# Issuing the float32 DFT matmuls of a fused FFT and MLP kernel in pairs

## The chip, the cores and the metric

The kernel runs on one core of a Trainium2 chip. The metric is the device time of one execution in microseconds (us). The engines are named as in the profile: PE (matmul), PEld (PE's weight loads), DVE (vector), ACT (activation), POOL (GpSimd) and SP, which issues the DMAs.

## The reference

A circular convolution along the sequence (by a real FFT, a product with a filter, and the inverse FFT) for 8 batches of 3008 x 256, and behind it a two-layer MLP with a rational activation on all 24064 rows.

```python
X = np.fft.rfft(x, axis=1)
Y = X * (filt_r + 1j * filt_i)[None, :, :]
y = np.fft.irfft(Y, n=x.shape[1], axis=1)
...
h = x @ w_in                      # 256 -> 2048
h2 = h * h; h3 = h2 * h
P = a[0] + a[1] * h + a[2] * h2 + a[3] * h3
Q = 1.0 + np.abs(b[0]) * np.abs(h) + np.abs(b[1]) * h2
return (P / (Q + 1e-06)) @ w_out  # 2048 -> 256
```

## The kernel before, in words

The FFT of length 3008 = 64 x 47 is made of small DFT matmuls in float32. Of one batch, stage 1 has 16 matmuls of 47 points (tiles `s`, 8 steps `q` with two halves `j` each, 96 x 512), stage 2 has 12 forward matmuls of 64 points (tiles `y`) and 12 inverse ones (tiles `z`), and stage 3 brings the result back with 47 points (tiles `x`, chunks of 5 small matmuls) and splits it into a high and a low part, `xh` and `xl`. The MLP's matmuls are fp32r with operands split into such parts.

The MLP goes in 752 units: 47 row tiles of 512 rows times 16 slices f of the hidden layer. The function `pipeline` has one step per unit. The engines run in the order in which it issues. In step i it issues, for PE, the six matmuls of `h` of unit i (L437, L438, L440: `product_in`), then at most one piece of convolution, then six matmuls `o` (L520 to L522: `product_out`) of the unit five steps back. Two of these are special: at f = 5 of each row tile no `o` is issued, since the two banks of `o` are still being copied out (`oe`), and at f = 6 there are two units' worth of `o`. A "step f" below is a step whose number is f modulo 16.

The elementwise work of a unit is spread over the later steps by `ORDER`: on DVE a step has g_hi of the unit two back (L497), then the DVE work of the convolution piece, then `rest` of the unit three back (L505), `p` of the last unit (L488) and g_lo of the unit three back (L511, which writes `lo_u`). At the end of the steps with f = 4 DVE also copies half of the last tile's output (`oe`, L250).

Convolution of batch b+1 runs while the MLP works on batch b. A generator (`stage1`, `stage2`) yields a price before each matmul (0.86), `pipeline` lets it go on when a credit is above zero, and the credit grows by 0.38 a step (0.6 for batch 1). After the matmul the generator yields; its evacuation is issued in the same step behind the first three names of `ORDER`. Pieces of stage 3 come in at f = 2 and 3 or f = 10 and 11, or a step later.

Six PSUM banks serve `h`, `s`, `y`, `z` and `x`. `Banks.tile` takes the free bank with the smallest key; `Banks.done` gives it back with the key "step + 0.5" for the convolution (issued with its evacuation) and "step + 1" for a unit, whose bank is given back at its g_lo, three steps after its `product_in`. So in every step four banks belong to units once `product_in` has taken its own, and two are free for the convolution. PE waits at a matmul until the last reader of the bank's former tile has finished.

Of the kernel before, what the change touches and what calls it, by code (L numbers as in the profile page):

```python
# [9 lines left out]
F32 = mybir.dt.float32  # L10
# [3 lines left out]
ALU = mybir.AluOpType  # L14
# [12 lines left out]
C = 256  # L27
# [13 lines left out]
WAITS = (0, 1)  # L41
ORDER = [('g_hi', 2), ('act3', 1), ('act0', 0), ('act4', 1), ('act2', 0), ('act1', 0), ('rest', 3), ('p', 1), ('g_lo', 3), ('pool_m', 2), ('pool_q1', 1), ('pool_q0', 0)]
EV1, EV2, EVO = "A", "AV", "AV"
# [14 lines left out]
TT = 512  # L58
# [45 lines left out]
def conv_moe(ctx: ExitStack, tc: tile.TileContext, xp, fr, fi, w_in, w_out, ab, mats, small, sgn, outT):  # L104
    nc = tc.nc
# [4 lines left out]
    conv = ctx.enter_context(tc.tile_pool(name="conv", bufs=2))  # L110
# [4 lines left out]
    sgn_sb = consts.tile([128, 32], F32, name="sgn_sb")  # L115
# [4 lines left out]
    mats_sb = consts.tile([128, 3, 128], F32, name="mats_sb")  # L120
# [25 lines left out]
    def square_scalars():  # L146

        x, y, z = col(6, 2), col(8, 2), col(10, 2)
        v.tensor_copy(col(6), A3)
        v.tensor_copy(col(7), B1)  # L150
        v.reciprocal(y, x)
        tt(out=z, in0=x, in1=y, op=ALU.mult)
        ts(out=z, in0=z, scalar1=-1.0, scalar2=2.0, op0=ALU.mult, op1=ALU.add)
        tt(out=y, in0=y, in1=z, op=ALU.mult)
        tt(out=SC, in0=A3, in1=col(9), op=ALU.mult)
        stt(out=PC, in0=A2, scalar=0.5, in1=col(8), op0=ALU.mult, op1=ALU.mult)
        stt(out=QC, in0=B0, scalar=0.5, in1=col(9), op0=ALU.mult, op1=ALU.mult)
        tt(out=P0, in0=A0, in1=col(8), op=ALU.mult)
        p1, q1, pc2, qc2 = (col(i) for i in range(10, 14))
        tt(out=p1, in0=A1, in1=col(8), op=ALU.mult)  # L160
        ts(out=q1, in0=col(9), scalar1=1.000001, scalar2=None, op0=ALU.mult)
        tt(out=pc2, in0=PC, in1=PC, op=ALU.mult)
        tt(out=qc2, in0=QC, in1=QC, op=ALU.mult)
        tt(out=PK, in0=p1, in1=pc2, op=ALU.subtract)
        tt(out=QK, in0=q1, in1=qc2, op=ALU.subtract)
# [77 lines left out]
    def rows(scr):  # L243
        return scr.rearrange("k (g m) c -> (k g) m c", m=NH)

    def evac(which, out, in_, i):
        if which[i % len(which)] == "A":
            nc.scalar.activation(out, in_, AF.Copy)
        else:
            nc.vector.tensor_copy(out, in_)  # L250
# [17 lines left out]
    def stage1_load(b, q):  # L268
        xin = conv.tile([R1, 2, TT], F32, tag="xin", name=f"xin{b}_{q}", bufs=XB)
        nc.sync.dma_start(  # L270
            xin.rearrange("p a b -> p (a b)"), xp[b, :, 4 * q : 4 * q + 4, :].rearrange("p m c -> p (m c)")
        )
        return xin

    def stage1(b, q, xin=None):

        if xin is None:
            xin = stage1_load(b, q)
        ev = conv.tile([R1, 2, TT], F32, tag="ev", name=f"s1e{b}_{q}")
        for j in range(2):  # L280
            yield 0.86
            k, pt = banks.tile(f"s1_{b}_{q}_{j}")
            nc.tensor.matmul(pt[:R1], a1_sb, xin[:, j], start=True, stop=True)  # L283
            yield
            evac(EV1, ev[:, j], pt[:R1], 2 * q + j)
            banks.done(k, 0.5)
        nc.sync.dma_start(
            rows(scr1[b])[:, 4 * q : 4 * q + 4, :].rearrange("r m c -> r (m c)"), ev.rearrange("p a b -> p (a b)")
        )

    class Stage2:
# [22 lines left out]
        def flat(self, v, j):  # L314
            return v[:, 2 * j : 2 * j + 2].rearrange("p k c -> p (k c)")

        def product(self, i):
            b, (q, j) = self.b, divmod(i, 2)
            yield 0.86
            bank, yt = banks.tile(f"y_{b}_{i}")  # L320
            nc.tensor.matmul(yt, mats_sb[:, 0, :], self.flat(self.tin[q], j), start=True, stop=True)  # L321
            yield
            self.z[i] = z, z2 = [self.flat(f_, j) for f_ in self.f[q]]

            def signed(k):
                return slice(k * C, k * C + C), sgn_sb[:, 2 * i + k : 2 * i + k + 1]

            if b == 0:

                for k in range(2):  # L330
                    cs, sg = signed(k)
                    nc.vector.scalar_tensor_tensor(
                        out=z2[:, cs], in0=yt[:, cs], scalar=sg, in1=z2[:, cs], op0=ALU.mult, op1=ALU.mult
                    )
                nc.vector.tensor_tensor(out=z, in0=yt, in1=z, op=ALU.mult)
                banks.done(bank, 0.5)
                return
            nc.vector.tensor_tensor(out=z2, in0=yt, in1=z2, op=ALU.mult)
            nc.vector.tensor_tensor(out=z, in0=yt, in1=z, op=ALU.mult)
            banks.done(bank, 0.5)  # L340

            zw = conv.tile([128, TT], F32, tag="zw", name=f"zw{b}_{i}")
            for o, n in ((1, 0), (0, 1)):
                o_, n_ = slice(64 * o, 64 * o + 64), slice(64 * n, 64 * n + 64)
                for k in range(2):
                    cs, sg = signed(k)
                    nc.gpsimd.tensor_scalar(
                        out=zw[o_, cs], in0=z2[n_, cs], scalar1=sg[n_], scalar2=1.0, op0=ALU.mult, op1=ALU.mult
                    )
                if WAITS[n]:  # L350
                    yield
            nc.gpsimd.tensor_tensor(out=z, in0=z, in1=zw, op=ALU.add)

        def inverse(self, i):
            b, (q, j) = self.b, divmod(i, 2)
            if j == 0:
                self.ev[q] = self.tl("ev", q)
            yield 0.86
            bank, zt = banks.tile(f"z_{b}_{i}")
            z, z2 = self.z.pop(i)  # L360
            nc.tensor.matmul(zt, mats_sb[:, 1, :], z, start=True, stop=b > 0)  # L361
            if b == 0:
                nc.tensor.matmul(zt, mats_sb[:, 2, :], z2, start=False, stop=True)
            yield
            evac(EV2 if b else "A", self.flat(self.ev[q], j), zt, i)
            banks.done(bank, 0.5)

        def store(self, q):
# [2 lines left out]
    def stage2(b):  # L371
        s = Stage2(b)
        for q in range(2):
            s.load_filter(q)
            s.load(q)
        for i in range(13):
            if i < 12:
                yield from s.product(i)
            if i > 0:
                yield from s.inverse(i - 1)  # L380
            if i % 2 == 0 and i // 2 + 2 < 6:
                s.load_filter(i // 2 + 2)
                s.load(i // 2 + 2)
            if i > 0 and i % 2 == 0:
                s.store(i // 2 - 1)
# [138 lines left out]
    banks = None  # L524
# [9 lines left out]
    def conv_items(b):  # L534
        for q in range(8):
            yield from stage1(b, q)
        for _ in range(GAP):
            yield
        yield from stage2(b)

    def run(gen):
        for _ in gen:
            pass
# [27 lines left out]
    def first_batch(squares):  # L571

        s = Stage2(0)
        xin = {}
        fl = iter(range(6))

        def do(tokens):
            for c in tokens:
                if c == "W":
                    dec.load()  # L580
                elif c == "D":
                    dec.step()
                elif c == "F":
                    s.load_filter(next(fl))

        for q in range(XB):
            xin[q] = stage1_load(0, q)
            do(H0[q])
            if q == 0:
                nc.sync.dma_start(small_sb, small)  # L590
                nc.sync.dma_start(mats_sb, mats)
                nc.sync.dma_start(sgn_sb[:, :K2], sgn)
                if squares:
                    square_scalars()
        for q in range(8):
            do(HA[q][0])
            run(stage1(0, q, xin.pop(q)))
            if q + XB < 8:
                xin[q + XB] = stage1_load(0, q + XB)
            do(HA[q][1])  # L600
        for q in range(XB - 1):
            s.load(q)
        for q in range(2):
            s.double_filter(q)
        for i in range(13):
            do(HB[i][0])
            if i < 12:
                run(s.product(i))
            if i > 0:
                run(s.inverse(i - 1))  # L610
            q, j = divmod(i, 2)
            if j == 0:
                if q + XB - 1 < 6:
                    s.load(q + XB - 1)
                if q > 0:
                    s.store(q - 1)
            elif q + 2 < 6:
                s.double_filter(q + 2)
            do(HB[i][1])
        for k in range(2):  # L620
            for _ in stage3(k):
                do(HC)
        do("W" * 16)
# [169 lines left out]
```

## Time and profile before

| | |
|---|---|
| device time, 3 runs | 2553.69 us median, 2551.76 to 2555.01 |
| profiled execution | 2553.93 us, span 2552.2 us |
| mean granted clock of PE | 0.987 of full speed |
| PE, DVE, ACT, POOL busy | 97%, 90%, 91%, 73% of the span |
| matmul records | 10712 (a float32 matmul has two records) |

The page gives the busy share of each engine and the chain of work that ended last. The views by line give groups of instructions with their mean duration; the timeline gives instructions in order of time with their start in us from the start of the span, their duration, and the idle time of the engine ahead of them where there was some. Neighbouring instructions of the same line are merged there ("x2"). The recorded duration of a matmul is longer than its share of PE, since matmuls overlap; what PE spends is read from one start to the next.

### The profile page before, as it was taken

Reading aid. Unit: us, or ns where it says so; the run is one execution under the profiler, and the core shown is the slowest. Engines: PE = TensorE matmul, PEld = TensorE weight load, DVE = VectorE, ACT = ScalarE, POOL = GpSimd, SP = SyncE. Lnnn points to the kernel's source line nnn. Section 1 sums busy time; section 2 is a strip of 40 time slices with the busy share of each in tenths; the row PEclk is TensorE's granted clock in tenths of the full one; section 3 lists DMA queues with packets and bytes.
Section 4 is the critical chain, followed back from the end, with each engine's and each line's share of the span. In section 5 each row is a group of like instructions: output and inputs, shape, how many; then the busy total and the mean of one; then the engine's idle time right before and its main releaser. Section 6 shows DMA issues by size and latency. Waiting matters only on the chain.

```text
span 2552.2 us, 35864 instructions
## 1 busy us (share of the span) xinstructions
PE 2485.2 (97%) x10712; PEld 1936.4 (76%) x10712; DVE 2284.9 (90%) x3560; ACT 2327.5 (91%) x4106; POOL 1865.5 (73%) x2032
## 2 busy tenths in 40 slices
PE   5699999999999999999999999999999999999998
PEld 1377777777777777777777777777777778888886
DVE  6869988899889998899888998899988999999998
ACT  4399899999999999999999999999999999999997
POOL 4457876788668876687657786688757877888887
PEclk8789999999999999999999999999999999999999
DMA  8733342333222332233313322233222210000000
GB/s 252 213 95 97 96 125 68 105 88 91 77 82 83 94 92 66 78 88 99 89 56 105 93 88 75 75 90 101 86 64 84 76 55 28 25 25 17 25 9 19
DMA packets 102781, 208.76 MB, mean 82 GB/s; under 512 B 8720, under 2 KB 58480, under 8 KB 102576
## 3 DMA queue, kind: packets, MB, share of 16 engines
q1 hardware_dynamic: 102576, 206.37, 27.1%
q8 instruction: 87, 1.43, 0.2%
q14 instruction: 118, 0.97, 0.1%
HBM read 131.36 MB, written 74.97 MB: 81 GB/s over the span
## 4 chain that ended last, share of the span: by engine, by line
PE 90%; DVE 4%; POOL 3%; ACT 1%; issue 1%; DMA 1%; SPq 0%; POOLq 0%; DVEq 0%; ACTq 0%
PE o L520 13%; PE o L521 13%; PE o L522 13%; PE h_u L438 13%; PE h_u L437 13%; PE h_u L440 12%; PE x L404 4%; PE s L283 4%; PE y L321 3%; PE z L361 3%; POOL q_u L502 2%; POOL q_u L483 1%; POOL a_u L471 1%; DMA raw<-w_in 0%; DVE dq L207 0%
## 5 line engine op out<-in xcount | busy, mean ns | idle before, releaser
L502 POOL TENSOR_TENSOR q_u<-q_u,hi_u 128x512 f32<-128x512 f32 x752 | 974.5, 1296 | 453.2 <-DVE hi_u L497 431.3
L520 PE MATMUL o<-hi_u,wo_sb 128*128 128x512 f32 x1504 | 701.2, 466 | 0.0
L497 DVE SCALAR_TENSOR_TENSOR hi_u<-h_u,scal,a_u 128x512 fp32r<-128x512 f32 x752 | 557.9, 742 | 70.2 <-ACT a_u L473 59.5
L505 DVE SCALAR_TENSOR_TENSOR h_u<-h_u,scal,q_u 128x512 f32<-128x512 f32 x752 | 564.2, 750 | 51.8 <-POOL q_u L502 51.0
L437 PE MATMUL h_u<-xh,wi_sb 128*128 128x512 f32 x1504 | 596.4, 397 | 5.5 <-ACT xh L413 4.0
L521 PE MATMUL o<-lo_u,wo_sb 128*128 128x512 f32 x1504 | 589.5, 392 | 0.9 <-DVE lo_u L511 0.9
L438 PE MATMUL h_u<-xl,wi_sb 128*128 128x512 f32 x1504 | 588.2, 391 | 1.2 <-DVE xl L415 1.2
L522 PE MATMUL o<-hi_u,wo_sb 128*128 128x512 f32 x1504 | 589.2, 392 | 0.0
L488 DVE SCALAR_TENSOR_TENSOR h_u<-w_u,scal,h_u 128x512 f32<-128x512 f32 x752 | 560.0, 745 | 0.0
L463 ACT ACTIVATE a_u<-q_u,scal 128x512 f32<-128x512 f32 x752 | 543.9, 723 | 0.0
L458 ACT ACTIVATE q_u<-q_u,scal 128x512 f32<-128x512 f32 x752 | 541.9, 721 | 1.9
L483 POOL TENSOR_SCALAR q_u<-q_u,scal 128x512 f32<-128x512 f32 x752 | 525.9, 699 | 2.9 <-ACT a_u L463 2.9
L445 ACT ACTIVATE q_u<-h_u 128x512 f32<-128x512 f32 x752 | 449.8, 598 | 81.8 <-PE h_u L440 55.4
L452 ACT ACTIVATE w_u<-h_u,scal 128x512 f32<-128x512 f32 x752 | 514.1, 684 | 0.0
L511 DVE TENSOR_TENSOR lo_u<-h_u,a_u 128x512 fp32r<-128x512 f32 x752 | 512.4, 681 | 0.1
L440 PE MATMUL h_u<-xh,wi_sb 128*128 128x512 f32 x1504 | 464.9, 390 | 0.0
L473 ACT ACTIVATE a_u<-a_u 128x512 f32<-128x512 f32 x688 | 433.5, 630 | 0.0
L520 PEld LDWEIGHTS o<-hi_u,wo_sb 128*128 128x128 f32 x1504 | 283.1, 188 | 112.8 <-issue 64.7
L521 PEld LDWEIGHTS o<-lo_u,wo_sb 128*128 128x128 f32 x1504 | 283.1, 188 | 111.3 <-issue 59.4
L437 PEld LDWEIGHTS h_u<-xh,wi_sb 128*128 128x128 f32 x1504 | 283.4, 188 | 72.8 <-ACT xh L413 4.3
L438 PEld LDWEIGHTS h_u<-xl,wi_sb 128*128 128x128 f32 x1504 | 283.5, 189 | 66.5 <-issue 4.1
L522 PEld LDWEIGHTS o<-hi_u,wo_sb 128*128 128x128 f32 x1504 | 282.5, 188 | 62.2
(80 smaller groups left out, 1985.7 us busy)
## 6 DMA issues: line engine op xcount, KB each, us to landing
xin<-xp SPq DMA_DIRECT2D x64, 384.0 KB, 3.7
scr<-s1e SPq DMA_DIRECT2D x64, 384.0 KB, 3.8
xin<-scr SPq DMA_DIRECT2D x48, 512.0 KB, 4.6
scr<-ev SPq DMA_DIRECT2D x48, 512.0 KB, 4.7
outT<-oe SPq DMA_DIRECT2D x47, 512.0 KB, 3.0
f<-fr SPq DMA_DIRECT2D x90, 256.0 KB, 4.2
f<-fi SPq DMA_DIRECT2D x90, 256.0 KB, 3.9
tl<-scr SPq DMA_DIRECT2D x45, 480.0 KB, 4.0
```

Of the source, the lines that this page charges most:

```text
L437: nc.tensor.matmul(o, w_in_part(0, f, cc), xh[:, cc, ts], start=cc == 0, stop=False)
L438: nc.tensor.matmul(o, w_in_part(0, f, cc), xl[:, cc, ts], start=False, stop=False)
L440: nc.tensor.matmul(o, w_in_part(1, f, cc), xh[:, cc, ts], start=False, stop=cc == 1)
L463: nc.scalar.activation(self.a, self.q, AF.Abs_reciprocal_sqrt, bias=QK)
L483: nc.gpsimd.tensor_scalar(out=self.q, in0=self.q, scalar1=1.0, scalar2=QK, op0=ALU.mult, op1=ALU.add)
L488: v.scalar_tensor_tensor(out=H, in0=w, scalar=PK, in1=H, op0=ALU.add, op1=ALU.mult)
L497: nc.vector.scalar_tensor_tensor(out=self.hi, in0=self.H, scalar=self.p0, in1=self.a, op0=ALU.add, op1=ALU.mult)
L502: nc.gpsimd.tensor_tensor(out=self.q, in0=self.q, in1=self.hi.bitcast(F32), op=ALU.mult)
L505: nc.vector.scalar_tensor_tensor(out=self.H, in0=self.H, scalar=self.p0, in1=self.q, op0=ALU.add, op1=ALU.subtract)
L520: nc.tensor.matmul(o, w_out_part(0, f, dd), self.hi, start=f == 0, stop=False)
L521: nc.tensor.matmul(o, w_out_part(0, f, dd), self.lo, start=False, stop=False)
L522: nc.tensor.matmul(o, w_out_part(1, f, dd), self.hi, start=False, stop=f == 15)
```

## The change

Batch 0, which runs ahead of the pipeline, is as before. From batch 1 on, one visit of the convolution to PE has two float32 matmuls where it had one. Stage 1 issues both halves of a step together, and evacuates the first in the same step and the second in the next one (`yield None`). Stage 2 issues the forward matmul i and the inverse matmul i-1 together (`both`), then the two DVE products of `y`, the evacuation of `z`, and the POOL work; the first forward and the last inverse matmul stay alone. The price of a visit is doubled to 1.72.

```diff
+        pts = []
+        yield 1.72
         for j in range(2):
-            yield 0.86
             k, pt = banks.tile(f"s1_{b}_{q}_{j}")
             nc.tensor.matmul(pt[:R1], a1_sb, xin[:, j], start=True, stop=True)
-            yield
+            pts.append((k, pt))
+        yield
+        for j, (k, pt) in enumerate(pts):
+            if j:
+                yield None
             evac(EV1, ev[:, j], pt[:R1], 2 * q + j)
             banks.done(k, 0.5)
...
+        def both(self, i):
+            b = self.b
+            yield 1.72 if 0 < i < 12 else 0.86
+            if i < 12:
+                bank, yt = self.forward(i)
+            if i > 0:
+                q, j = divmod(i - 1, 2)
+                if j == 0:
+                    self.ev[q] = self.tl("ev", q)
+                zbank, zt = banks.tile(f"z_{b}_{i - 1}")
+                nc.tensor.matmul(zt, mats_sb[:, 1, :], self.z.pop(i - 1), start=True, stop=True)
             yield
...
+            if i < 12:
+                z, z2 = [self.flat(f_, i % 2) for f_ in self.f[i // 2]]
+                self.z[i] = z
+                nc.vector.tensor_tensor(out=z2, in0=yt, in1=z2, op=ALU.mult)
                 nc.vector.tensor_tensor(out=z, in0=yt, in1=z, op=ALU.mult)
                 banks.done(bank, 0.5)
+            if i > 0:
+                evac(EV2, self.flat(self.ev[q], j), zt, i - 1)
+                banks.done(zbank, 0.5)
...
         for i in range(13):
-            if i < 12:
-                yield from s.product(i)
-            if i > 0:
-                yield from s.inverse(i - 1)
+            yield from s.both(i)
```

PE in step 197 (f = 5) of the kernel before. Here `h_u_7415` is unit 197, `y_1_7422` the forward matmul of this step, and `h_u_7447` unit 198; no `o` stands between them.

```order
L437 MATMUL h_u_7415<-xh,wi_sb 128x512
L438 MATMUL h_u_7415<-xl,wi_sb 128x512
L437 MATMUL h_u_7415<-xh,wi_sb 128x512
L438 MATMUL h_u_7415<-xl,wi_sb 128x512
L440 MATMUL h_u_7415<-xh,wi_sb 128x512 x2
L321 MATMUL y_1_7422<-xin_0_7240,mats_sb 128x512
L437 MATMUL h_u_7447<-xh,wi_sb 128x512
```

The next unit's `h` follows the single float32 matmul here.

PE in the same step of the changed kernel: `h_u_7451` is unit 197, `h_u_7487` unit 198.

```order
L454 MATMUL h_u_7451<-xh,wi_sb 128x512
L455 MATMUL h_u_7451<-xl,wi_sb 128x512
L454 MATMUL h_u_7451<-xh,wi_sb 128x512
L455 MATMUL h_u_7451<-xl,wi_sb 128x512
L457 MATMUL h_u_7451<-xh,wi_sb 128x512 x2
L325 MATMUL y_3_7458<-xin_1_7058,mats_sb 128x512
L353 MATMUL z_2_7461<-f_1_7052,mats_sb 128x512
L454 MATMUL h_u_7487<-xh,wi_sb 128x512
```

An inverse matmul now stands behind the forward one, and the `h` of the next unit follows the two directly. By the keys of `Banks` it takes the bank of `y_3_7458`.

PE in step 310 (f = 6) of the changed kernel, from the unit's last `h` matmuls on.

```order
L457 MATMUL h_u_11284<-xh,wi_sb 128x512 x2
L325 MATMUL y_8_11291<-xin_4_10730,mats_sb 128x512
L353 MATMUL z_7_11293<-f_3_10440,mats_sb 128x512
L537 MATMUL o_0_11295<-hi_u_11162,wo_sb 128x512
L538 MATMUL o_0_11295<-lo_u_11214,wo_sb 128x512
```

Between the `h` and the `o` of this step PE now has a forward and an inverse matmul.

DVE of the changed kernel from the middle of step 309, which has no convolution, to the middle of step 310.

```order
L522 SCALAR_TENSOR_TENSOR h_u_11149<-h_u_11149,scal,q_u_11166 128x512
L505 SCALAR_TENSOR_TENSOR h_u_11218<-w_u_11242,scal,h_u_11218 128x512
L528 TENSOR_TENSOR lo_u_11280<-h_u_11149,a_u_11165 128x512
L514 SCALAR_TENSOR_TENSOR hi_u_11309<-h_u_11218,scal,a_u_11240 128x512
L358 TENSOR_TENSOR f_4_10725<-y_8_11291,f_4_10725 128x512
L359 TENSOR_TENSOR f_4_10724<-y_8_11291,f_4_10724 128x512
L250 COPY ev_3_11116<-z_7_11293 128x512
```

The matmul `z_7_11293` takes the bank of unit 306, whose last reader is the g_lo that writes `lo_u_11280` (it reads `h_u_11149`), issued one step earlier. Before, a convolution matmul or an `h` in this place took a bank of a g_lo issued two steps earlier, and the evacuation of `z` had a step of its own.

## Rows read from the trace of the kernel before

**Rows 1.** The page: the span, the busy time of four engines (us, share of the span, instructions), and the chain of work that ended last by engine.

```profile
span 2552.2 us, 35864 instructions
...
PE 2485.2 (97%) x10712; PEld 1936.4 (76%) x10712; DVE 2284.9 (90%) x3560; ACT 2327.5 (91%) x4106; POOL 1865.5 (73%) x2032
...
PE 90%; DVE 4%; POOL 3%; ACT 1%; issue 1%; DMA 1%; SPq 0%; POOLq 0%; DVEq 0%; ACTq 0%
```

**Rows 2.** The waits of PE between 140 and 2400 us: who waited for whom, us in total, times, longest.

```profile
PE x L404 <- DVE xl L415: 0.2, 1, 0.2
PE y L321 <- DVE ev L250: 0.2, 1, 0.2
```

**Rows 3.** The groups of PE by line and shape over the whole span: the float32 matmuls of the stages 1 and 2 (count of records; busy us, mean ns of one; idle before).

```profile
L283 PE MATMUL s<-xin,small_sb 96*96 96x512 f32 x256 | 133.7, 611 | 13.3 <-DMA small_sb<-small 9.6 <-DMA xin<-xp 2.0 <-ACT s1e L248 1.3
...
L321 PE MATMUL y<-xin,mats_sb 128*128 128x512 f32 x192 | 100.7, 607 | 16.8 <-DMA xin<-scr 16.6 <-DVE ev L250 0.2
L361 PE MATMUL z<-f,mats_sb 128*128 128x512 f32 x192 | 100.5, 605 | 10.5 <-issue 9.4 <-ACT f L308 1.2
```

**Rows 4.** The timeline of PE between 600 and 640 us. A single `z` stands between the second and the third row with L521; the rows from 634.69 on stand around a single `s` in the same way.

```profile
604.28 0.39 PE L521 MATMUL o<-lo_u,wo_sb 128*128 128x512 f32 x1
...
606.77 1.02 PE L361 MATMUL z<-f,mats_sb 128*128 128x512 f32 x2
...
607.86 0.40 PE L521 MATMUL o<-lo_u,wo_sb 128*128 128x512 f32 x1
...
610.62 0.39 PE L521 MATMUL o<-lo_u,wo_sb 128*128 128x512 f32 x1
...
634.69 0.39 PE L521 MATMUL o<-lo_u,wo_sb 128*128 128x512 f32 x1
...
638.27 0.40 PE L521 MATMUL o<-lo_u,wo_sb 128*128 128x512 f32 x1
...
641.02 0.39 PE L521 MATMUL o<-lo_u,wo_sb 128*128 128x512 f32 x1
```

**Rows 5.** The timeline of PE in batch 0, where float32 matmuls follow one another (two records each).

```profile
54.34 1.02 PE L321 MATMUL y<-xin,mats_sb 128*128 128x512 f32 x2
55.20 1.02 PE L361 MATMUL z<-f,mats_sb 128*128 128x512 f32 x2
56.06 1.02 PE L363 MATMUL z<-f,mats_sb 128*128 128x512 f32 x2
56.92 1.02 PE L321 MATMUL y<-xin,mats_sb 128*128 128x512 f32 x2
```

**Rows 6.** The timeline around step 197 (f = 5, from 779.82 us): an `x` in the step before it, a `y` in it, no `o` behind it; the step 198 begins with the row at 781.81.

```profile
777.31 1.25 PE L404 MATMUL x<-small_sb,tl 96*128 96x96 f32 x10
...
779.82 0.39 PE L437 MATMUL h_u<-xh,wi_sb 128*128 128x512 f32 x1
...
781.08 0.68 DVE L511 TENSOR_TENSOR lo_u<-h_u,a_u 128x512 fp32r<-128x512 f32 x1
781.18 1.02 PE L321 MATMUL y<-xin,mats_sb 128*128 128x512 f32 x2
781.68 0.68 DVE L250 COPY oe<-o 128x512 f32<-128x512 f32 x1
781.81 0.62 PE L437 MATMUL h_u<-xh,wi_sb 128*128 128x512 f32 x1
...
782.27 0.74 DVE L497 SCALAR_TENSOR_TENSOR hi_u<-h_u,scal,a_u 128x512 fp32r<-128x512 f32 x1
...
782.93 0.68 DVE L338 TENSOR_TENSOR f<-y,f 128x512 f32<-128x512 f32 x1
...
783.53 0.68 DVE L339 TENSOR_TENSOR f<-y,f 128x512 f32<-128x512 f32 x1
...
785.44 0.68 DVE L511 TENSOR_TENSOR lo_u<-h_u,a_u 128x512 fp32r<-128x512 f32 x1
```

**Rows 7.** The timeline around step 613 (f = 5, from 2141.77 us), with no convolution in the steps 612 to 614: step 612 begins at 2139.05, step 614 at 2143.13. The rows with L511 are the g_lo of the steps 612 and 613.

```profile
2139.05 0.39 PE L437 MATMUL h_u<-xh,wi_sb 128*128 128x512 f32 x1
...
2141.77 0.39 PE L437 MATMUL h_u<-xh,wi_sb 128*128 128x512 f32 x1
...
2142.88 0.68 DVE L511 TENSOR_TENSOR lo_u<-h_u,a_u 128x512 fp32r<-128x512 f32 x1
...
2143.13 0.39 PE L437 MATMUL h_u<-xh,wi_sb 128*128 128x512 f32 x1
...
2143.48 0.68 DVE L250 COPY oe<-o 128x512 f32<-128x512 f32 x1
...
2144.49 0.39 PE L520 MATMUL o<-hi_u,wo_sb 128*128 128x512 f32 x1
...
2146.05 0.68 DVE L511 TENSOR_TENSOR lo_u<-h_u,a_u 128x512 fp32r<-128x512 f32 x1
```

More of the change, by code (lines that the diff above doesn't have):

```diff
@@ L315, in flat, with forward @@
             return v[:, 2 * j : 2 * j + 2].rearrange("p k c -> p (k c)")
-        def product(self, i):
[L318 to L321, printed above, removed]
-            yield
[L323 to L334, printed above, removed]
+        def forward(self, i):
+            q, j = divmod(i, 2)
+            bank, yt = banks.tile(f"y_{self.b}_{i}")
+            nc.tensor.matmul(yt, mats_sb[:, 0, :], self.flat(self.tin[q], j), start=True, stop=True)
+            return bank, yt
@@ new lines, in signed @@
+        def signed(self, i, k):
+            return slice(k * C, k * C + C), sgn_sb[:, 2 * i + k : 2 * i + k + 1]
+        def product(self, i):
+            q, j = divmod(i, 2)
+            bank, yt = self.forward(i)
+            self.z[i] = z, z2 = [self.flat(f_, j) for f_ in self.f[q]]
+            for k in range(2):
+                cs, sg = self.signed(i, k)
+                nc.vector.scalar_tensor_tensor(
+                    out=z2[:, cs], in0=yt[:, cs], scalar=sg, in1=z2[:, cs], op0=ALU.mult, op1=ALU.mult
+                )
+            nc.vector.tensor_tensor(out=z, in0=yt, in1=z, op=ALU.mult)
+            banks.done(bank, 0.5)
@@ new lines, in both @@
+        def both(self, i):
+            b = self.b
+            yield 1.72 if 0 < i < 12 else 0.86
+            if i < 12:
+                bank, yt = self.forward(i)
+            if i > 0:
[4 more added lines that the diff above has]
+                nc.tensor.matmul(zt, mats_sb[:, 1, :], self.z.pop(i - 1), start=True, stop=True)
+            yield
+            if i < 12:
+                z, z2 = [self.flat(f_, i % 2) for f_ in self.f[i // 2]]
+                self.z[i] = z
+                nc.vector.tensor_tensor(out=z2, in0=yt, in1=z2, op=ALU.mult)
@@ L335, in product @@
                 nc.vector.tensor_tensor(out=z, in0=yt, in1=z, op=ALU.mult)
                 banks.done(bank, 0.5)
[L337 to L351, printed above, removed]
@@ L352, in product @@
-            nc.gpsimd.tensor_tensor(out=z, in0=z, in1=zw, op=ALU.add)
+            if i > 0:
+                evac(EV2, self.flat(self.ev[q], j), zt, i - 1)
+                banks.done(zbank, 0.5)
+            if i < 12:
+                zw = conv.tile([128, TT], F32, tag="zw", name=f"zw{b}_{i}")
+                for o, n in ((1, 0), (0, 1)):
+                    o_, n_ = slice(64 * o, 64 * o + 64), slice(64 * n, 64 * n + 64)
+                    for k in range(2):
+                        cs, sg = self.signed(i, k)
+                        nc.gpsimd.tensor_scalar(
+                            out=zw[o_, cs], in0=z2[n_, cs], scalar1=sg[n_], scalar2=1.0, op0=ALU.mult, op1=ALU.mult
+                        )
+                    if WAITS[n]:
+                        yield
+                nc.gpsimd.tensor_tensor(out=z, in0=z, in1=zw, op=ALU.add)
@@ L357, in inverse @@
                 self.ev[q] = self.tl("ev", q)
-            yield 0.86
             bank, zt = banks.tile(f"z_{b}_{i}")
             z, z2 = self.z.pop(i)
[L361 to L365, printed above, removed]
+            nc.tensor.matmul(zt, mats_sb[:, 1, :], z, start=True, stop=False)
+            nc.tensor.matmul(zt, mats_sb[:, 2, :], z2, start=False, stop=True)
+            evac("A", self.flat(self.ev[q], j), zt, i)
             banks.done(bank, 0.5)
@@ L607, in first_batch @@
             if i < 12:
-                run(s.product(i))
+                s.product(i)
             if i > 0:
-                run(s.inverse(i - 1))
+                s.inverse(i - 1)
             q, j = divmod(i, 2)
```

## The prediction

> **What bounds the kernel now.** I read the page first: PE is busy 97% of the span and makes 90% of the chain that ended last [rows 1]. DVE (90%) and ACT (91%) are not far behind, so the second view is the list of PE's own waits. Between 140 and 2400 us it holds two entries of 0.2 us [rows 2]. So nearly all of the span is a stream of matmuls without holes: a microsecond taken out of PE's stream is gained in full, and a microsecond of waiting put into it is lost in full, because nothing ahead of it is slack that could take it up. The third view, the groups by line, says how much float32 work there is in the two stages: 256 records of `s`, 192 of `y`, 192 of `z`, two to a matmul [rows 3]; batch 0 has an eighth of the matmuls and isn't touched. The timeline then has to answer two questions: what a visit of float32 costs beyond its own length, and how late DVE is with the banks that the second matmul of a pair needs.
>
> **What a pair saves on PE.** From L521 at 604.28 to `z` at 606.77 are 11 fp32r matmuls, 2.49 us, so 0.226 us each, and a step of 12 without float32 takes 2.72 us. The stretch with a `z` goes from 604.28 to 607.86, 3.58 us: 0.86 more. The step behind it, 607.86 to 610.62, takes 2.76, so 0.04 us more than a plain one although it holds no float32: matmuls shortly after a float32 one come a little slower. A single `z` costs 0.90 us. For `s` the same three rows give 3.58 and 2.75, 0.89 us [rows 4]. Where float32 matmuls follow one another, one costs 0.86: from 54.34 to 56.92 are three of them, and changing the weights between `y` and `z` costs nothing visible [rows 5]. The second matmul of a pair thus costs 0.86 instead of 0.90 or 0.89. Per batch there are 11 pairs of `y` with `z` and 8 of `s`; over 7 batches 77 x 0.04 + 56 x 0.03 = 4.8 us. With rows rounded to 0.01 the term lies between 3 and 7 us. That the slower matmuls behind a pair cost twice as much as behind a single one would take it to zero; `s` and `z`, equally long, already differ in it, so I keep 4.8.
>
> **What moves on the other engines.** ACT and POOL do the same instructions as before. On DVE, half of the `z` evacuations (0.59 us from start to start, as the copy of `oe` between 781.68 and 782.27 [rows 6]) now follow the products in one step, but a step with a pair lasts 2.72 + 1.72 = 4.44 us on PE, so DVE gets more time in it than it has work. SP's stores and loads of the stages come a step earlier or later, with several steps of cover. The start-up (before 140 us) has one pair in another order ahead of the first `o`; its matmuls are the same, I take 0 and allow 2 us either way.
>
> **What the pairs wait for.** The banks are the new thing. Two are free in a step; one matmul took the older and left the other to the next unit, so every bank rested at least a step more than needed. A pair takes both. Its second matmul gets the bank of the unit four back, whose g_lo DVE has issued only one step earlier, and the next unit's `h` gets the bank of the pair's first matmul, evacuated in this very step. On PE's time, counted from the start of a step: `h` ends at 1.36, the second matmul of the pair wants to begin at 1.36 + 0.86 = 2.22, and the next `h` at 4.44, or at 1.36 + 1.72 = 3.08 where there is no `o`.
>
> In an ordinary step this is enough. After a step with an `x`, the g_lo of that step ends at 781.08 + 0.68 = 781.76, that is 1.94 us into the next step, which began at 779.82 [rows 6]; 2.22 is later by 0.28. The products of `y` end some 3.7 us into a step (`y` ends at 2.4, two products 1.28), well ahead of 4.44. So I take 0 for the ordinary pairs; the 0.28 is thin, and the bound on that side is a rival below.
>
> It isn't enough around the step f = 5 without `o`. Following the issue order of the changed kernel, pairs fall into the following places.
>
> First, pairs in f = 6: nine (steps 54, 86, 102, 262, 310, 358, 374, 534, 582). The step before lasts only 1.36 us on PE, while DVE has a full step and a copy of `oe` in it. In the plain case the g_lo of f = 5 ends at 2146.05 + 0.68 = 2146.73, 3.60 us into the step f = 6, which began at 2143.13 [rows 7]. The second matmul of a pair wants that bank at 2.22: a wait of 1.4 us. That row has a plain step at f = 4; its own g_lo ended 2143.56, 1.79 into the next. In five of the nine an `x` stands at f = 4, which leaves 1.94 [rows 6], so they wait 1.55 us each, 7.8 in all. In 54 and 102 a pair of `y` and `z` stands at f = 4: DVE, 1.94 behind from an `x` at f = 3, does a step with the products of `y`, which takes it 3.85 us (782.27 to 785.44 + 0.68 [rows 6]), and leaves at 1.94 + 3.85 - 4.44 = 1.35, or at 1.95 where the copy of `z` is DVE's, as in 54; 1.8 more at f = 5 as above, so waits of 1.6 and 1.0. In 374 a single `y` stands there: 1.94 + 3.85 - 3.58 = 2.2, a wait of 1.8. In 262 a pair of `s` gives DVE time, and I take 0. Sum 12.2 us.
>
> Second, pairs in f = 5: five with `y` (37, 133, 197, 229, 405). The next `h` wants the bank of `y` at 3.08. In the step 197 of before, the second product began at 783.53 and ended at 784.21, 4.39 us into the step [rows 6]: DVE comes from the `x`, copies `oe`, does g_hi and only then the products. The `h` that follows waits 1.35 us with the signal. Four such and one that is 0.15 shorter make 6.6 us. Six pairs of `s` in f = 5 hand on a bank that ACT empties; a few tenths at most, 0.5 in all.
>
> The sum: 2553.93 (the profiled execution) - 4.8 + 12.2 + 6.6 + 0.5 = 2568.4 us. This execution is 0.2 above the median of the three, so 2568 stands for either.
>
> That a `z` which waits holds up more than itself is seen in its place in the order: six or twelve `o` stand behind it. The plain step shows such an `o` start at 2144.49, 1.36 us after `h`, without a wait [rows 7]; it could run and would not be let past. The Trainium skill, "TensorE: Matmul & The Clock Gate", section "Part 3: Packing small matmuls — row/col tiling", says of this that matmuls start and end in program order and only weight loads are pulled ahead; no row here contradicts it. The Trainium skill, "Perfetto Trace Analysis", section "Identifying Performance Opportunities", says that a gap that repeats on the engine which should be saturated can mean that too few buffers are left for the next tile. The trace of before shows no such gap; by the rule the pairs would bring one at each row tile, and without it the sum would be 2549.
>
> **Rivals.**
> 1. The waits don't come, and the saved switches are all there is: 2553.93 - 4.8 = 2549. For it speaks that in the same steps of before PE never waited; against it, that before no matmul there used a bank of the step before. It would need DVE to be 1.4 us earlier than in the rows, for instance because the longer pair steps let it catch up everywhere.
> 2. The waits come at half the size: DVE, given a pair's 4.44 us a step or two earlier, is less late in f = 4 and 5 than in rows 6 and 7. 2553.93 - 4.8 + 9.7 = 2559, at the edge of no change. Against it: lateness after an `x` is set anew by the time at which `x` itself is done.
> 3. The thin cover of the ordinary pairs breaks: 0.28 us behind an `x`, some 0.6 elsewhere. With POOL's product late, DVE's `rest` slips, and each of the remaining 110 or so pairs waits 0.15 us more: 2568 + 16 = 2584. It decides from a lateness of 2.22 us at the start of a pair's step.
>
> **How the numbers follow.** The forecast has a chance of 0.60, rival 1 0.13, rival 2 0.18, rival 3 0.09. The predicted time is 2568, and the forecast's own range is 2560 to 2576 (the two families of waits each a third smaller or larger, the start-up, the saved term between 3 and 7). The range reaches to rival 1 on one side and half way to rival 3 on the other: 2550 to 2578. What the measurement can tell from no change is about 0.2%, or 5.1 us: 2548.6 to 2558.8. Rival 1 falls on the lower edge of this: I give 0.10 to faster, 0.22 to about the same (the rest of rival 1 and half of rival 2), and 0.68 to slower.
>
> **What would show it.** In the profile after, PE's waits should hold some 14 entries on DVE, at L353 and L284 behind g_lo (L528) in the steps f = 6, and at L454 behind the product of `y` (L359) in the steps f = 5, of 1 to 1.8 us each and 15 to 22 us in all. The pairs should run 0.86 us per matmul from start to start. Outside those steps PE should have no waits over 0.2 us. A list without these entries, or a time under 2557, makes the account of the banks wrong; more than 30 entries make it too narrow.

## The result and the profile after

The changed kernel takes 2577.23 us (median of 6 runs, 2576.45 to 2577.89), the kernel before 2553.89 us on the same chip (6 runs, 2550.95 to 2556.91): ratio 1.0092, 95% interval 1.0079 to 1.0105. It is slower by 23 us. The forecast was 2568, the range 2550 to 2578. The profiled execution took 2576.45 us. The times of the experiments are medians too, and one execution of one of them, at 12083 us, is left out of its median.

The page of the changed kernel, the same parts as in [rows 1]:

```profile
span 2574.7 us, 35871 instructions
...
PE 2488.7 (97%) x10712; PEld 1933.3 (75%) x10712; DVE 2286.1 (89%) x3560; ACT 2314.8 (90%) x4106; POOL 1867.1 (73%) x2032
...
PE 83%; DVE 5%; POOL 4%; ACT 2%; issue 2%; POOLq 0%; DVEq 0%; ACTq 0%
```

The busy times of all engines are within 1% of before, and the span is 22.5 us longer: the same work with holes in it. PE's share of the chain that ended last fell from 90% to 83%; the shares of DVE, POOL, ACT and "issue" grew by one point each. Where the holes are is said by the list of PE's waits between 140 and 2400 us (us in total, times, longest), which held 0.4 us before [rows 2]:

```profile
PE h_u L454 <- DVE f L359: 6.0, 5, 1.3
PE s L284 <- DVE lo_u L528: 5.2, 4, 1.5
PE z L353 <- DVE lo_u L528: 4.3, 4, 1.6
PE z L353 <- POOL f L375: 3.0, 2, 1.6
PE x L421 <- DVE xl L432: 0.9, 1, 0.9
PE z L353 <- POOL q_u L519: 0.8, 2, 0.4
PE z L353 <- issue: 0.2, 1, 0.2
```

Five waits of `h` for the product of `y`, and ten of `z` or `s` for a g_lo (the two put down to POOL's add at L375 among them; an experiment below shows that they are DVE's).

One wait of the first kind, from the timeline of step 197, where before `h` followed at once [rows 6]:

```profile
792.32 1.02 PE L325 MATMUL y<-xin,mats_sb 128*128 128x512 f32 x2
793.17 1.02 PE L353 MATMUL z<-f,mats_sb 128*128 128x512 f32 x2
...
794.66 0.68 DVE L359 TENSOR_TENSOR f<-y,f 128x512 f32<-128x512 f32 x1
795.40 0.50 PE L454 MATMUL h_u<-xh,wi_sb 128*128 128x512 f32 x1 [1.21 <-DVE f L359]
```

`h` takes the bank of `y`, whose second product ends at 794.66 + 0.68 = 795.34; `h` starts 0.06 us later. From `z` to `h` are 2.23 us, where a `z` has 0.86.

One wait of the second kind, step 310, which begins with the first row. The step before it is the one without `o`:

```profile
1161.49 0.39 PE L454 MATMUL h_u<-xh,wi_sb 128*128 128x512 f32 x1
...
1162.85 1.02 PE L325 MATMUL y<-xin,mats_sb 128*128 128x512 f32 x2
...
1164.67 0.68 DVE L528 TENSOR_TENSOR lo_u<-h_u,a_u 128x512 fp32r<-128x512 f32 x1
...
1165.50 1.10 PE L353 MATMUL z<-f,mats_sb 128*128 128x512 f32 x2 [1.64 <-DVE lo_u L528]
...
1166.04 0.80 PE L537 MATMUL o<-hi_u,wo_sb 128*128 128x512 f32 x1
```

The g_lo that empties `z`'s bank ends at 1165.35, 3.86 us into the step; the prediction's sum of rows gave 3.60 plus 0.15 behind an `x`. `z` starts at 1165.50 instead of 1162.85 + 0.86 = 1163.71. The idle time in the row is 1.64 us, but the start is 1.79 late: the row counts idle from the recorded end of `y`, and a recorded duration (1.02) is longer than PE's share (0.86). So the waits below are measured from start to start. The 19 waits of the list, 20.4 us as recorded, come to about 25 us that way, and the losses of pairs that show no idle time in a row add some 4.

A pair that waits for nothing, from L538 to L538:

```profile
488.55 0.39 PE L538 MATMUL o<-lo_u,wo_sb 128*128 128x512 f32 x1
...
491.04 1.02 PE L325 MATMUL y<-xin,mats_sb 128*128 128x512 f32 x2
491.90 1.02 PE L353 MATMUL z<-f,mats_sb 128*128 128x512 f32 x2
492.36 0.79 PE L537 MATMUL o<-hi_u,wo_sb 128*128 128x512 f32 x1
492.99 0.40 PE L538 MATMUL o<-lo_u,wo_sb 128*128 128x512 f32 x1
...
495.75 0.39 PE L538 MATMUL o<-lo_u,wo_sb 128*128 128x512 f32 x1
```

It takes 4.44 us and the next step 2.76, 1.76 more than two plain steps of 2.72. Two single visits cost 2 x 0.90 [rows 4]: 0.04 is saved, as forecast.

### The profile page after: what moved, and what is told of

Read it like the earlier page. It is cut to its first block, busy times and chain, and to the rows that moved or that the text cites. A ratio compares the mean times of both kernels' runs of the same rounds, so it can differ in the third digit from the quotient of the medians.

```text
span 2574.7 us, 35871 instructions
## 1 busy us (share of the span) xinstructions
PE 2488.7 (97%) x10712; PEld 1933.3 (75%) x10712; DVE 2286.1 (89%) x3560; ACT 2314.8 (90%) x4106; POOL 1867.1 (73%) x2032
## 4 chain that ended last, share of the span: by engine, by line
PE 83%; DVE 5%; POOL 4%; ACT 2%; issue 2%; POOLq 0%; DVEq 0%; ACTq 0%
PE o L537 12%; PE o L539 12%; PE o L538 12%; PE h_u L454 12%; PE h_u L455 12%; PE h_u L457 12%; PE x L421 4%; PE s L284 3%; PE z L353 3%; PE y L325 2%; POOL q_u L519 2%; POOL q_u L500 1%; DVE h_u L522 1%; POOL a_u L488 1%; DVE h_u L505 1%
## 5 line engine op out<-in xcount | busy, mean ns | idle before, releaser
L537 PE MATMUL o<-hi_u,wo_sb 128*128 128x512 f32 x1504 | 651.5, 433 | 0.0
L522 DVE SCALAR_TENSOR_TENSOR h_u<-h_u,scal,q_u 128x512 f32<-128x512 f32 x752 | 564.6, 751 | 47.6 <-POOL q_u L519 46.8
L538 PE MATMUL o<-lo_u,wo_sb 128*128 128x512 f32 x1504 | 587.2, 390 | 0.8 <-DVE lo_u L528 0.8
L539 PE MATMUL o<-hi_u,wo_sb 128*128 128x512 f32 x1504 | 587.8, 391 | 0.0
L538 PEld LDWEIGHTS o<-lo_u,wo_sb 128*128 128x128 f32 x1504 | 283.3, 188 | 85.6 <-issue 32.8
```

The lines of the kernel that those rows point to most:

```text
L522: nc.vector.scalar_tensor_tensor(out=self.H, in0=self.H, scalar=self.p0, in1=self.q, op0=ALU.add, op1=ALU.subtract)
L537: nc.tensor.matmul(o, w_out_part(0, f, dd), self.hi, start=f == 0, stop=False)
L538: nc.tensor.matmul(o, w_out_part(0, f, dd), self.lo, start=False, stop=False)
L539: nc.tensor.matmul(o, w_out_part(1, f, dd), self.hi, start=False, stop=f == 15)
```

## The experiments

Unless said otherwise each is an edit of the changed kernel, and "expected" was on record before the run.

**Where the visits stand.** The condition under which `pipeline` lets a visit start excludes f = 5 and f = 6:

```diff
-            elif credit > 0 and i < n and not active ...
+            elif credit > 0 and f not in (5, 6) and i < n and not active ...
```

> The pairs stay, but none may start in a step f = 5 or f = 6; they move to f = 7 and f = 4. Theory (the second matmul of a pair and the next h wait for banks around the step without o): the waits of 13 us in f = 6 and of 8 us in f = 5 go, the few tenths at distance three stay, and the 27 pairs now in f = 7 may wait some tenths each: 2554 to 2562 us. Rival (a pair costs PE about 0.2 us wherever it stands, by its length or by what it does to ACT and POOL): the same number of pairs, so 2574 to 2580 us.

Measured: 2563.38 us, ratio 1.0041 (1.0027 to 1.0055). The waits of f = 5 and 6 are gone, and more than half of the loss with them; the time is 1.4 us above what was expected. PE's waits left between 140 and 2400 us:

```profile
PE x L421 <- DMA tl<-scr: 4.3, 1, 4.3
PE z L353 <- DVE lo_u L528: 1.3, 3, 0.7
PE s L284 <- DVE lo_u L528: 0.8, 1, 0.8
PE z L353 <- POOL q_u L519: 0.7, 1, 0.7
PE o L538 <- DVE lo_u L528: 0.5, 2, 0.3
```

The pairs that moved to f = 7 are not free: from start to start 14 of the 27 lose 0.1 to 1.0 us each, 5.2 us in all. The long wait of `x` has a place of its own, as the same edit of the kernel before shows.

> Control: the kernel before, with single matmuls, whose visits are kept out of f = 5 and f = 6 in the same way. If moving the visits has no price of its own, 2552 to 2558 us (there is one step with three matmuls in batch 1, at most 3 us). If the steps 5 and 6 are good places for a single float32 matmul, because PE has less to do in f = 5, it is slower by more, 2560 us and up; then a gain of the first run would be understated.

Measured: 2564.74 us, ratio 1.0047 (1.0031 to 1.0063): the control alone costs 12 us and missed its expectation. All of it stands in two steps, 73 and 74 (3.4 and 8.5 us, the second with PE at half its clock for a part, see the last section), at the end of batch 1's convolution. PE's waits between 140 and 2400 us in this control:

```profile
PE x L404 <- DMA tl<-scr: 6.3, 1, 6.3
PE z L361 <- POOL f L352: 3.1, 1, 3.1
PE x L404 <- DVE xl L415: 0.2, 1, 0.2
```

Batch 1 has no slack: with fewer places for its visits the last ones are crowded, and stage 3 waits for its load. The changed kernel with the edit has a loss of the same sort, 7.5 us at steps 66 and 67. So leaving f = 5 and 6 free costs nothing per single visit, but what it does to batch 1 has to be kept apart.

**More pairs in f = 6.** The opposite edit, `f not in (3, 4, 5)`, puts 33 pairs into f = 6, where nine stood.

> The suspected wait made more frequent: pairs may not start in f = 3, 4 or 5, so 33 of the 133 pairs fall into f = 6 instead of 9, none into f = 5. Theory: 33 waits of 1.0 to 1.8 us (those without an x or y shortly ahead less) instead of 13 us in f = 6 and 8 in f = 5: 2577 - 21 + 33 x 1.3 = 2599 us, between 2585 and 2612. Rival (a price per pair wherever it stands): 2574 to 2580 us.

Measured: 2607.32 us, ratio 1.0220 (1.0203 to 1.0237), as expected. PE's waits in it, between 140 and 2400 us:

```profile
PE z L353 <- DVE lo_u L528: 19.0, 17, 1.5
PE s L284 <- DVE lo_u L528: 18.0, 13, 1.5
PE z L353 <- POOL q_u L519: 11.0, 10, 1.6
```

From start to start 32 of the 33 lose 1.5 to 1.8 us each, 52 us in all; that of step 6, in the first row tile, where no output is copied yet, loses nothing. The price of a pair in f = 6 holds wherever one is put there later, for `s` as for `z`. Ten waits are put down to POOL's q_u here, seven of them in f = 6; which engine was late at these was not tested.

**Stage 1 alone in pairs.** Stage 2 is as before, with `product` and `inverse` in visits of their own.

> Only stage 1 is paired (56 pairs); y and z go singly as before. Seven of the pairs start in f = 5 and two in f = 6. Theory: 1.5 us saved on PE, 2 x 1.7 us of waits in f = 6 and 7 x 0.3 us in f = 5, and nothing from the product of y: 2553.9 - 1.5 + 5.5 = 2558 us, 2553 to 2561. Rival (a price per pair): 56 of 133 pairs bring 56/133 of 23 us, 2564 us.

Measured: 2558.51 us, ratio 1.0023 (1.0013 to 1.0032), as expected; the two `s` pairs that now fall into f = 6 lose 1.65 and 1.77 us. They and that of step 21 are the waits at a g_lo:

```profile
PE s L284 <- DVE lo_u L548: 3.8, 3, 1.5
...
```

The pairs in f = 5 did not lose 0.3 us each: that of step 69 lost 0.8, behind ACT, and that of step 21 about 1.4. `s` has no DVE product, so it is the bank and not DVE's extra work in a visit that makes the wait.

**DVE's copy of `oe` taken away.** Both halves of the output tile are copied by ACT:

```diff
-EV1, EV2, EVO = "A", "AV", "AV"
+EV1, EV2, EVO = "A", "AV", "A"
```

> The changed kernel with both halves of the output copy oe on ACT, so that DVE has no copy between f = 4 and f = 5 and is 0.59 us less late there. Theory (the waits in f = 5 and f = 6 are DVE's lateness): each of the 13 long waits is about 0.5 to 0.6 us shorter; the pairs of s in f = 5, which wait for ACT, wait up to 0.5 us longer: 2577 - 7 + 2 = 2571 us, 2568 to 2574. Rival (the short step on PE alone sets the wait, whatever DVE does): 2576 to 2579 us.

> Control for the run before it: the kernel before with both halves of oe on ACT. No wait of PE rests on it there, so 2552 to 2556 us; if ACT or DVE mattered by itself it would be off by more than 4 us.

Measured: 2571.11 us, ratio 1.0067 (1.0052 to 1.0083), and for the control on the kernel before 2553.29 us, ratio 1.0002 (0.9992 to 1.0011). So the copy costs nothing by itself, and without it the changed kernel is 6 us faster by the medians; the two intervals of the ratio just overlap, so the waits have to show it. PE's longest waits in the first of the two, between 140 and 2400 us:

```profile
PE s L284 <- DVE lo_u L528: 3.4, 4, 0.9
PE z L353 <- DVE lo_u L528: 3.3, 4, 1.0
PE h_u L454 <- DVE f L359: 3.0, 5, 0.7
...
```

The five waits of f = 5 fell from 6.0 to 3.0 us, by the 0.6 us that the copy takes on DVE. In f = 6 most fell by as much, those of 102 and 374 by 0.11 and 0.16 only. Two `s` pairs in f = 5 lose 0.5 more, behind ACT, which has the copy now. DVE's lateness is the cause, and in most of the places the copy is a good third of it.

**Pairs kept four steps apart.** Batch 1 is as before the change. From batch 2 on pairs come in no f = 5 or 6, and at least four steps after the last visit.

```diff
-            elif credit > 0 and i < n and not active ...
+            elif credit > 0 and (nxt < 2 or f not in (5, 6) and i >= lastp + 4) and i < n and not active ...
```

> Pairs where no bank is late: batch 1 single as before, from batch 2 on pairs only at least 4 steps apart and never in f = 5 or 6; by the issue order they fall on f = 0, 4, 8 and 12 nearly always (114 pairs). Theory: no waits of PE beside those of before, and the saved switches remain, 66 x 0.04 + 48 x 0.03 = 4.1 us: 2549 us, 2547 to 2552, 0.16% under the kernel before. Rival (a pair has a price wherever it stands): 114/133 of 23 us on top, 2573 us.

Measured: 2550.67 us, ratio 0.9991 (0.9982 to 1.0000). Within the expected span, with half of the gain. PE's waits left between 140 and 2400 us:

```profile
PE z L369 <- DVE lo_u L601: 2.1, 4, 0.8
PE x L494 <- DVE xl L505: 0.7, 1, 0.7
```

Four pairs in f = 11 and 14 still wait. **Every fourth step** puts the visits from batch 2 on at `f % 4 == 0` (rate 0.44 instead of 0.38, batch 1 as before):

> As the run with pairs at least 4 steps apart, but from batch 2 on a visit may only start at f = 0, 4, 8 or 12, and the credit grows by 0.44, so that the batches end in time. The run before had waits of 0.6 to 1.2 us left at five places (f = 6, 7, 11, 14). Theory: these go too, 2552.8 - 4 = 2549 us (2547 to 2551), faster than the kernel before by 0.15%. Rival (a fixed rhythm makes ACT or DVE late at the same steps each time): new waits at f = 0 or 4, 2553 us or more.

Measured: 2551.3 us, ratio 0.9990 (0.9981 to 0.9999). The median is just outside what was expected, and the gain of 0.1% is less than the 0.2% that a measurement can tell from no change. Three pairs wait, all at f = 12 and 0.9 to 1.1 us each:

```profile
PE z L369 <- DVE lo_u L601: 2.2, 3, 0.8
```

These two are the only versions with pairs that are not slower than the kernel before. By the medians some 2 us were got there, of the 4 that 114 pairs at 0.04 us could save; neither measurement tells that from no change.

**The short waits.** Apart from those of f = 5 and 6, the changed kernel has short ones: 15 pairs lose 0.1 to 0.7 us each. One of them is step 287, from the timeline (it begins at 1086.23):

```profile
1080.25 1.97 POOL L370 TENSOR_SCALAR zw<-f,sgn_sb 64x256 f32<-64x256 f32 x4
...
1084.25 1.31 POOL L375 TENSOR_TENSOR f<-f,zw 128x512 f32<-128x512 f32 x1
1085.51 1.31 POOL L519 TENSOR_TENSOR q_u<-q_u,hi_u 128x512 f32<-128x512 f32 x1
...
1086.85 0.76 DVE L522 SCALAR_TENSOR_TENSOR h_u<-h_u,scal,q_u 128x512 f32<-128x512 f32 x1 [0.55 <-POOL q_u L519]
...
1088.17 0.69 DVE L528 TENSOR_TENSOR lo_u<-h_u,a_u 128x512 fp32r<-128x512 f32 x1
...
1089.01 1.10 PE L353 MATMUL z<-f,mats_sb 128*128 128x512 f32 x2 [0.39 <-POOL q_u L519]
```

Read from the bottom: `z` waits for a bank that g_lo leaves at 1088.86. DVE was late there since `rest` (L522) had waited 0.55 us for POOL's q_u, and q_u stood behind the add of the last pair's product. In the first run the add (L375) is left out from batch 1 on:

```diff
-                nc.gpsimd.tensor_tensor(out=z, in0=z, in1=zw, op=ALU.add)
```

In the second, made later, the four small products ahead of it (`zw`, L370) go too.

> The changed kernel without POOL's last addition to z in the batches past the first (the mixed half zw is computed and not added, so the output lacks that term from batch 1 on). POOL has 1.24 us less to do behind each of the 84 y. Theory (the short waits at f = 0, 1, 7, 9, 10, 13 and 15, some 4 us, come from POOL, which holds up rest on DVE when a pair follows three steps after another): these go, the 13 long waits in f = 5 and 6 stay: 2573 us, 2571 to 2575. Rival (they are DVE's own lateness): they stay as they are, 2576 to 2579 us.

> The changed kernel without any POOL work of stage 2 from batch 1 on: the four small products of a step (zw, 1.97 us on POOL) and the add to z (1.31 us) are both left out, so that the inverse matmuls work on half of the product; matmuls, DVE and ACT are as in the changed kernel. Theory (the short waits of ordinary pairs that the run without the add left, at steps 29, 191, 215, 282, 461 and 553, are there because zw stands ahead of q_u on POOL and holds up DVE's rest): all six go, nothing else in PE's stream changes, the five waits at L454 of f = 5 stay at 1.3 (6.0 us in all) and those of f = 6 lose 0.1 at most: 1.5 to 2 us less than the run without the add, 2571 to 2573 by the median. Rival (DVE is late there by its own work, POOL only shows as the last releaser): the six waits stay at 0.2 to 0.5, time as without the add, 2574. Rival (POOL is also what makes DVE late in f = 5 and 6): the long waits shrink by 0.3 us or more each, 2569 or less.

Measured without the add: 2573.86 us, ratio 1.0082 (1.0067 to 1.0098). The waits at f = 0 and 1 and in 31, 287, 559 are gone, those in 29, 191, 215, 282, 461, 553 stay: the time is as expected, the list only in part. Without both: 2572.38 us, ratio 1.0074 (1.0057 to 1.0091), and five of the six are gone; the one at 215, 0.2 us, stays. PE's waits in this second run, between 140 and 2400 us:

```profile
PE z L353 <- DVE lo_u L520: 6.5, 5, 1.6
PE h_u L446 <- DVE f L359: 6.0, 5, 1.3
PE s L284 <- DVE lo_u L520: 5.2, 4, 1.5
PE x L413 <- DVE xl L424: 0.9, 1, 0.9
```

The long waits of f = 5 and 6 are what they were, and those of `z` that the trace of the changed kernel put down to POOL's add are now put down to DVE: 9 long waits at g_lo, and five of 1.3 us at the product. POOL has next to no part in the long waits (from start to start none of them is shorter by more than 0.07 us), and nearly the whole one in the short ones. The five were worth 1.6 us; the intervals of these two runs and of the changed kernel overlap, so it is the list and not the time that shows it.

## Why the prediction was right, and what it missed

**Saved switches, 4.8 us.** Right. 47 pairs of `y` and `z` that wait for nothing take 4.44 us and 2.77 for the next step, 33 pairs of `s` 4.45 and 2.73. That is 0.04 us saved per pair, 5 us for 133 pairs. The matmuls behind a pair are slower by no more than those behind a single one.

**Pairs in f = 6, 12.2 us.** Right in place and cause, a little small. From start to start the nine named steps lose 1.59, 1.66, 1.03, 0.08, 1.87, 1.78, 1.85, 1.66 and 1.75 us (54, 86, 102, 262, 310, 358, 374, 534, 582): 13.3 us. The forecast had 1.6, 1.55, 1.0, 0, 1.55, 1.55, 1.8, 1.55, 1.55. Part of the rest is that a `z` which has waited runs 0.08 us longer.

**Pairs of `y` in f = 5, 6.6 us.** Right: 1.5 us in 37, 133 and 197, 1.6 in 405, 1.3 in 229, 7.4 in all. The six pairs of `s` there were put at 0.5, which was too little: four of them lose 0.1 to 0.4 us each, 1.0 in all, and that in step 21 about 1.3 us. That one waits for a g_lo and not for ACT. In the first row tile the step without `o` is step 20 and not f = 5, so step 21 stands where f = 6 does in the others; it begins at 197.59 us, behind the start-up for which 2 us were allowed.

**The step that failed** is "So I take 0 for the ordinary pairs". It cost 4.8 us, in 15 pairs. With it failed the sign that outside f = 5 and 6 no wait would be over 0.2 us: those of 282, 287 and 464 have 0.35 to 0.44 in their rows. The cover was worked out for a pair behind an `x` or a plain step, from the trace of before, in which a `y` follows two steps behind another 5 times. In the changed kernel it does so 19 times, in the stretches in which the convolution catches up, and 14 of the 15 pairs stand two or three steps behind the last `y`; then POOL's work for one product stands ahead of the next q_u, DVE's `rest` waits for it, and g_lo leaves the bank later than 2.22 us into the step. That is rival 3's mechanism, but it hit 15 pairs and not 110. A further 1.2 us is an `x` at step 550 that waits for the bank of another `x`; no step of the prediction spoke of it.

Together: 13.3 + 7.4 + 1.0 + 1.3 + 4.8 + 1.2 - 5 = 24.0 us, against 22.5 us between the two spans. The 1.5 us between them are not traced.

**The range.** Every term of the waits came out larger than forecast, nearly 10 us together, and only 0.2 us more of saving went the other way. The time is above the forecast's own range of 2560 to 2576 and 0.8 us under the upper end of 2578. Half way from 2568 to rival 3's 2584 is 2576; the 2 us beyond it, which let the measured time in, come from no term of the sum. The places and the cause were foreseen; that the time still fell inside the range is luck.

**The rivals.** Rival 1 (no waits, 2549) is out by the list of waits; the two versions that put the pairs elsewhere come within 2.5 us of its time, so it is about the time of this change without its waits. Rival 2 (half the waits) is out: they came at 1.1 times the forecast size. The Trainium skill, "Perfetto Trace Analysis", section "Identifying Performance Opportunities", says that a gap which repeats on the engine that should be saturated can mean that too few buffers are left for the next tile. The trace agrees, with 14 gaps of 1.0 to 1.9 us, but only in the row tiles in which a pair falls on f = 5 or 6. The others have the same six banks and, but for the `x` at step 550, no such gap.

Not tried was a seventh bank, or another key for the banks. That either would end the waits is argued from the order alone.

## What to carry to other kernels

Before work is bunched on a saturated engine, list for each buffer it takes in the new order who empties it and how many steps earlier that was issued: here a rest of a step was what absorbed DVE's lateness, and issuing two matmuls together spent it. The saving per bunch (0.04 us) has to be set against one wait (1 to 1.9 us): one pair in forty on the wrong step eats it all. Placing the pairs where the elementwise engine is on time took the loss away here, and of the small saving no more than the noise allows to see. So when such a change loses, look first at where its pieces stand.

## What the runs showed of the hardware that was not expected

**The clock can fall behind a wait.** In the run without POOL's work of stage 2, step 358 lost 3.4 us, where the changed kernel lost 1.8 there. Its timeline on PE:

```profile
1320.71 1.10 PE L284 MATMUL s<-xin,small_sb 96*96 96x512 f32 x2 [1.54 <-DVE lo_u L520]
...
1322.69 0.63 PE L529 MATMUL o<-hi_u,wo_sb 128*128 128x512 f32 x1
1323.12 0.63 PE L530 MATMUL o<-lo_u,wo_sb 128*128 128x512 f32 x1
```

After a wait of 1.54 us the `o` matmuls start 0.43 us apart, where 0.23 is usual. The busy times by window (from and to, length, five engines, then the granted clock) have the clock at half, 1.2 GHz:

```profile
1323.00:1325.00 2.00, 2.00 (x6) 1.54 (x6) 0.96 (x3) 0.68 (x2) 0.42 (x1) 0.50 0.00 0
```

It was back at full speed at about 1325.3. The same wait of 1.54 us at step 358 of the changed kernel, and of the run without the add, left the granted clock at 1.00. In the run with f = 5 and 6 left out, a wait of 4.33 us for a load was followed by half speed too:

```profile
356.80:358.50 1.70, 1.70 (x8) 1.70 (x9) 0.00 (x0) 0.00 (x0) 0.00 (x0) 0.50 0.23 58
358.50:362.80 4.30, 4.30 (x12) 3.43 (x12) 3.28 (x6) 2.94 (x6) 0.00 (x0) 0.50 0.01 2
```

So of the 7.5 us lost there some 3 are the clock's, since 6.0 us went at half speed. In its control the granted clock was 0.50 from 381.6 to 388.3 us, around the end of the wait of 6.28 us for a load. But the 32 losses of 1.5 to 1.8 us in the run with more pairs in f = 6, and the 14 long ones of the changed kernel, left the granted clock at 1.00 over 140 to 2400 us. Why the clock fell behind one wait of that length out of so many is open, and that the wait made it fall is not shown.

**A late matmul is also slower.** A `z` or `s` that has waited has 1.10 us in its row where others have 1.02, and the `o` behind it starts 0.54 us after it (1165.50 to 1166.04) instead of 0.46 (491.90 to 492.36). With the idle time understated in the rows, a list of 19 waits of 20.4 us stood for about 25 us.
